# Layer two's second product as seven block products over transposed operands, with the SBUF slots divided by use

## The chip, the cores and the metric

One core of one Trainium2 chip runs the kernel. The metric is device time in microseconds (us) for one execution; lower is better. A profile of one execution gives the rows below. PE is TensorE, DVE is VectorE, ACT is ScalarE, POOL is GpSimd, SP is the engine that issues most DMAs. A "512 matmul" streams 512 columns through a 128x128 weight block.

## The reference

```python
x = attention(q, k_pooled, v_pooled)               # (8, 8, 576, 64) -> 4608 x 512
h = x @ w_in                                       # w_in 512 x 2048
x = (h * (1 / (1 + exp(-1.702 * h)))) @ w_out      # layer one, w_out 2048 x 512
out = ((x @ w_a) * (x @ w_b)) @ w_out2             # layer two, w_a, w_b 512 x 1536, w_out2 1536 x 512
```

Everything is FP32. Each product is made of three matmuls in the rounded FP32 format fp32r: every operand is split in a high part and a low remainder (hi, lo), and hi·hi, hi·lo and lo·hi are summed in PSUM.

## The kernel before

**Units and passes.** The 4608 tokens are nine blocks of 512. Four pairs of blocks and the last block by itself make five units u = 0..4. Work goes through passes i over the hidden columns; in a pass all units are done one after the other. The first phase (attention and a direct layer one) is followed by passes that do layer one with block products, and then by the last three passes, LP, LP+1 and LP+2, which are layer two. Each of these takes four chunks f of 128 hidden columns (f0 to f3 below), of the 12 that there are.

**The first product of layer two** is done in seven block products for eight. The four quarters of x of a unit are combined beforehand into seven operands `xo` (hi and lo, in DRAM as `yd`), the weights of each chunk into seven blocks `wc` (in DRAM as `wd`). `products` runs, for a unit and a chunk, P1, P5, P6, P3, P7, P2, P4, six matmuls each (L837), into PSUM tiles X (two buffers), Y and Z. ACT copies the sums of P1, P5 and P6 out, DVE adds those of P3, P7, P2 and P4, and multiplies the two halves of the gate: L866 after P7 gives column half 1, L871 after P4 column half 0. L814 (ACT) and L815 (DVE) split these into hi and lo.

**The second product** is direct. `out_rows` takes 128 tokens as the stationary operand and a weight tile `wo` (512 columns) as the moving one, three matmuls (L751, L752, L753) per 128 tokens and chunk, into an accumulator of the pool `acc`. These groups stand in a list; an entry On in a table (FIRST_F for a pass's first chunk, OTHER_F) lets n of them run between two products. The first half of them can run while the first product of the next chunk goes on; those of column half 0 run at the end of the pass, during the next unit.

**Sums over passes.** LP writes its part of the result to DRAM (`part`), LP+1 reads and rewrites it, LP+2 reads it and stores the output. So READS holds LP+1 and LP+2. `evict` copies an accumulator out (L941 on ACT, L943 on DVE) or adds the loaded part (L933, DVE), and stores it (L944): by SP in READS, by POOL in LP.

**Order.** The order on PE is fixed by the program (`after_last`). On the other engines a scheduler decides it from its own estimates before the run, and each engine then executes its list strictly in that order.

**Weights of layer two** are converted on the way (`pieces_ab`, `whole`: ACT L1088, DVE L1089 to L1106, then a split and a store). The chunks needed in pass LP+1 are made during LP, those of LP+2 during LP+1, with 512 KB loads on SP.

**Slots.** One pool of 19 slots of 1 MB, tag "w", holds xo, wc, wo, raw words and results in the making.

## Time and profile before

| what | value |
|---|---|
| median of three runs | 1736.1 us (1735.93 to 1737.71) |
| span of the profiled execution | 1732.5 us |
| median of the runs less that span | 3.6 us |
| PE busy | 1717.8 us, 99% of the span |
| DVE busy | 1055.2 us, 61% |
| ACT busy | 682.9 us, 39% |
| POOL busy | 38.5 us, 2% |
| HBM traffic over the span | 247 GB/s |

The span runs from the first to the last instruction of the profiled execution. What a run takes beyond it is start and end of the program, 3.6 us with the median. Busy shares are means over stages with different limits.

### The profile page before, as it was taken

How to read it: one execution, taken by the hardware profiler on the slowest of the kernel's cores; microseconds unless marked ns; L12 is line 12 of the kernel's file. 1: busy time of each engine (PE TensorE's matmuls, PEld its weight loads, DVE VectorE, ACT ScalarE, POOL GpSimd, SP SyncE). 2: the span in 40 equal slices, each digit the busy share in tenths (PEclk: the TensorE clock that was granted, in tenths of full speed). 3: DMA queues.
4: the chain of work that ended last, by engine and by line, in shares of the span. 5: the costliest groups of instructions: out<-in, count | busy, mean ns of one | idle time of the engine just before them, and what ended most of it. 6: DMA issues, size and time to landing. Idle time of an engine off the chain costs nothing.

```text
span 1732.5 us, 23390 instructions
## 1 busy us (share of the span) xinstructions
PE 1717.8 (99%) x8708; PEld 1435.9 (83%) x8708; DVE 1055.2 (61%) x1791; ACT 682.9 (39%) x1624; POOL 38.5 (2%) x69
## 2 busy tenths in 40 slices
PE   9999999999999999999999999999999999999999
PEld 8888887888888888888888888888888888888888
DVE  8999866675846644665555547643547753444443
ACT  8977643553323344544542223322223222222111
POOL 0000000000100000000000100000000000000000
PEclk9999999999999999999999999999999999999999
DMA  7776566465936994756868756598556879735612
GB/s 295 244 272 242 173 213 240 158 240 199 353 125 265 373 377 169 285 193 220 322 237 349 276 201 256 229 373 324 219 214 221 339 298 411 281 123 213 243 58 89
DMA packets 122913, 429.35 MB, mean 248 GB/s; under 512 B 12976, under 2 KB 17584, under 8 KB 99888
## 3 DMA queue, kind: packets, MB, share of 16 engines
q1 hardware_dynamic: 116320, 401.39, 62.5%
q0 software_dynamic: 6480, 26.48, 4.0%
q8 instruction: 68, 1.11, 0.3%
q14 instruction: 45, 0.37, 0.1%
HBM read 286.52 MB, written 141.30 MB: 247 GB/s over the span
## 4 chain that ended last, share of the span: by engine, by line
PE 87%; DVE 6%; DMA 4%; ACT 3%; issue 1%; SPq 0%; ACTq 0%; DVEq 0%
PE X L837 20%; PE Y L837 10%; PE acc L753 6%; PE acc L751 6%; PE acc L752 6%; PE Z L837 5%; PE h L338 4%; PE acc L338 4%; PE acc L340 4%; PE acc L339 4%; PE h L339 4%; PE h L340 4%; PE acc L767 2%; PE acc L766 2%; PE acc L765 2%; DMA yd<-st 2%
## 5 line engine op out<-in xcount | busy, mean ns | idle before, releaser
L837 PE MATMUL X<-xo,wc 128*128 128x512 f32 (+1 forms) x1800 | 410.1, 368 | 1.7 <-ACT s L845 1.7
L837 PEld LDWEIGHTS X<-xo,wc 128*128 128x128 f32 x1800 | 318.7, 188 | 62.6 <-ACT s L845 3.2
L837 PE MATMUL Y<-xo,wc 128*128 128x512 f32 (+1 forms) x900 | 209.2, 368 | 0.0
L837 PEld LDWEIGHTS Y<-xo,wc 128*128 128x128 f32 x900 | 159.2, 188 | 28.6
L851 DVE TENSOR_TENSOR s<-s,Y 128x512 f32<-128x512 f32 (+1 forms) x75 | 47.5, 634 | 169.8 <-PE Y L837 169.6
L338 PE MATMUL h<-x,w 128*128 128x512 f32 x360 | 143.1, 399 | 3.3 <-ACT x L615 2.8
L814 ACT CAST ghi<-s 128x512 fp32r<-128x512 f32 (+1 forms) x90 | 52.0, 578 | 234.3 <-DVE s L866 204.8
L339 PE MATMUL h<-x,w 128*128 128x512 f32 x360 | 140.3, 390 | 0.2 <-DVE x L617 0.2
L339 PE MATMUL acc<-glo,w 128*128 128x512 f32 x360 | 140.3, 390 | 0.2 <-DVE glo L1275 0.2
L340 PE MATMUL h<-x,w 128*128 128x512 f32 x360 | 140.4, 390 | 0.0
L340 PE MATMUL acc<-ghi,w 128*128 128x512 f32 x360 | 140.3, 390 | 0.0
L338 PE MATMUL acc<-ghi,w 128*128 128x512 f32 x360 | 131.6, 398 | 0.4 <-ACT ys L1297 0.3
L814 ACT CAST hi<-s 128x512 fp32r<-128x512 f32 (+1 forms) x90 | 51.5, 578 | 147.0 <-DVE s L871 146.6
L837 PE MATMUL Z<-xo,wc 128*128 128x512 f32 (+1 forms) x450 | 104.5, 368 | 0.0
L571 ACT ACTIVATE at<-sc,mx 128x72 f32<-128x72 f32 x288 | 88.5, 345 | 24.9 <-DVE mx L564 24.8
L837 PEld LDWEIGHTS Z<-xo,wc 128*128 128x128 f32 x450 | 80.0, 188 | 14.8
L753 PE MATMUL acc<-wo,glo 128*128 128x512 f32 x216 | 84.4, 391 | 0.6 <-DVE glo L815 0.6
L751 PE MATMUL acc<-wo,ghi 128*128 128x512 f32 x216 | 84.5, 391 | 0.0
L752 PE MATMUL acc<-wo,hi 128*128 128x512 f32 x216 | 84.3, 390 | 0.0
L751 PE MATMUL acc<-wo,hi 128*128 128x512 f32 x216 | 84.3, 390 | 0.0
L752 PE MATMUL acc<-wo,ghi 128*128 128x512 f32 x216 | 84.3, 390 | 0.0
L753 PE MATMUL acc<-wo,lo 128*128 128x512 f32 x216 | 84.0, 389 | 0.0
(116 smaller groups left out, 3027.0 us busy)
## 6 DMA issues: line engine op xcount, KB each, us to landing
xo<-yd SPq DMA_DIRECT2D x84, 1024.0 KB, 9.1
yd<-st SPq DMA_DIRECT2D x126, 256.0 KB, 3.0
part<-part SPq DMA_DIRECT2D x108, 256.0 KB, 5.0
part<-part SPq DMA_DIRECT2D x19, 1024.0 KB, 7.7
xd<-x SPq DMA_DIRECT2D x18, 1024.0 KB, 7.5
xm<-xd SPq DMA_DIRECT2D x32, 512.0 KB, 8.2
raw<-in_moe_w_out_dram SPq DMA_DIRECT2D x28, 512.0 KB, 7.9
wd<-ws SPq DMA_DIRECT2D x12, 1024.0 KB, 4.1
```

Source lines behind the costliest of these rows:

```text
L338: nc.tensor.matmul(out=o, lhsT=whi, rhs=xhi, start=first, stop=False),
L339: nc.tensor.matmul(out=o, lhsT=whi, rhs=xlo, start=False, stop=False),
L340: nc.tensor.matmul(out=o, lhsT=wlo, rhs=xhi, start=False, stop=last),
L571: pin("ACT", nc.scalar.activation(out=a[:, h, :], in_=sc[:, c, :], func=AF.Exp, bias=mx[:, h:h + 1], accum_out=sm[:, h:h + 1],))
L751: after_last(nc.tensor.matmul(out=oa, lhsT=chi[:, ts], rhs=whi, start=first, stop=False))
L752: after_last(nc.tensor.matmul(out=oa, lhsT=chi[:, ts], rhs=wlo, start=False, stop=False))
L753: after_last(nc.tensor.matmul(out=oa, lhsT=clo[:, ts], rhs=whi, start=False, stop=last))
L765: after_last(nc.tensor.matmul(out=oa, lhsT=whi, rhs=chi, start=first, stop=False))
L766: after_last(nc.tensor.matmul(out=oa, lhsT=wlo, rhs=chi, start=False, stop=False))
L814: nc.scalar.copy(out=chi, in_=src)
L837: after_last(nc.tensor.matmul(out=banks[nm], lhsT=w[we][:, ks], rhs=x[:, xe, kk, :], start=n in FIRST and kk == 0 and m == 0, stop=kk == 1 ...
L851: made = nc.vector.tensor_tensor(out=s[2], in0=s[2], in1=Y, op=ALU.add)
```

## The change

The second product of layer two is computed transposed: the weights are stationary, the tokens are the moving side, and it goes through seven block products as well, now over pairs p of chunks. A unit has 14 groups, two for each product (one per pair of chunks), called k0 to k13 here. Each group computes two accumulators (r = 0, 1) with three matmuls each: 84 matmuls for a unit, of 512 columns, or 256 for the last unit, instead of 96 (48) of 512. The tokens' side of a group is made by `ready`: four subtractions on DVE for each pair of chunks, and a split (ACT cast, DVE subtract) for each group. The weights' side is made with the other weights (seven blocks, `wd["o", n]`).

The running sums of the block products are read in the middle: after each odd k, `add_out` (L954; in LP the first time L952, a copy on ACT) adds the two accumulators to a quarter of the result, and a later group goes on accumulating in the same PSUM banks: k4 continues in the two banks of Y that are read after k3, k8 in those of X that are read after k1. The additions after k7, k9, k11 and k13 end a quarter each, which is then stored by ACT's own DMA queue. In a unit that is 14 additions, 8 subtractions and 14 splits on DVE.

Other parts of the change: the next unit's xo are loaded as soon as their slot is free, at the end of each product of f3 (`load_operand`), instead of earlier into other slots; parts are loaded in quarters (`load_quarter`, L945: column 1 of rows 2 and 3 in f2, column 0 and column 1 of rows 0 and 1 in f3, the last two after k7); 126 stores of `yd` go from SP to POOL; weights of chunks 0 to 4 are made in the first phase, those of 5 to 11 one quarter at a time by `made_late`, with POOL loads and stores through two small tiles `spare`, spread from LP's second chunk to the end of LP+1; the 19 slots become 14 of "w", 4 of "wo", 1 of "v". The result is stored transposed and turned outside the kernel.

```diff
-ROOM = dict(ps=4, acc=3, at=2, aT=4, tmp=2, g=1, gg=2, ks=4, raws=2, vs=2, q=2, xs=3, raw=2, yp=2, w=19)
+ROOM = dict(ps=4, acc=3, at=2, aT=4, tmp=2, g=1, gg=2, ks=4, raws=2, vs=2, q=2, xs=3, raw=2, yp=2, w=14, wo=4, v=1)
...
-            t = wp.tile([P, 2, 2, N], F32R, tag="w", name="xo")
+            t = big("v" if i == L2 - 1 and n == 0 else "w", [P, 2, 2, N], F32R, "xo")
...
-    def out_rows(i, f, col, ti, j, c, first, last):
...
-        whi, wlo = w[:, f % 2, :], w[:, 2 + f % 2, :]
-        ts = slice(ti * P, (ti + 1) * P)
...
-        after_last(nc.tensor.matmul(out=oa, lhsT=chi[:, ts], rhs=whi, start=first, stop=False))
-        after_last(nc.tensor.matmul(out=oa, lhsT=chi[:, ts], rhs=wlo, start=False, stop=False))
-        after_last(nc.tensor.matmul(out=oa, lhsT=clo[:, ts], rhs=whi, start=False, stop=last))
...
+                if not one_ and u + 1 < NU2:
+                    load_operand(i, u + 1, USED.index(o))
...
-                held[1, f] = col_tiles(gp, 2, "ghi", "glo")
-                parts(held[1, f], s[1])
+                held[i, u, f, 1] = s[1]
...
+        if last and not one_:
+            ready, sweep_ = sweep(i, u)
...
+            elif what[0] == "L":
+                for c, col in LOADED[what] if i in READS else ():
+                    load_quarter(i, u, c, col)
...
-        groups.extend(g for _, g in rows_of(1, f, held.pop((1, f))))
         if last:
-            per_f = [list(rows_of(0, f_, held.pop((0, f_)))) for f_ in fs]
-            for ti in range(n_ // P):
-                groups.extend(p[ti][1] for p in per_f)
...
+    SWEEP = (1, 5, 3, 2, 6, 7, 4)
+    ADDS = {1: (0, 0), 5: (1, 1), 3: (0, 1), 2: (0, 0), 6: (0, 1), 7: (1, 1), 4: (1, 0)}
+    ENDS = (2, 6, 7, 4)
...
+            for to, x, y in {3: (((0, 0), (0, 1), (0, 0)),),
+                             4: (((0, 1), (1, 1), (0, 1)), ((1, 1), (1, 1), (0, 0))),
+                             6: (((1, 0), (1, 0), (1, 1)),)}.get(o, ()):
+                nc.vector.tensor_tensor(out=b(*to), in0=b(*x), in1=b(*y), op=ALU.subtract)
+            e, col = ((0, 0), (1, 0), (1, 1), (0, 0), (1, 1), (0, 1), (1, 0))[o]
+            xs[k_] = pair_tiles(n_, (k_ if final else made_ops[0]) % ahead < 2)
+            made_ops[0] += 1
+            split(*xs[k_], b(e, col))
...
+            for r in range(2):
+                if n in (1, 5) and k_ % 2 == 0:
+                    banks[bank_, r] = acc.tile([P, n_], F32, tag="acc", name="acc")
+                o_ = banks[bank_, r]
+                whi, wlo = (wo[:, e, r * P:(r + 1) * P] for e in range(2))
+                for m, (w_, x_) in enumerate(((whi, hi), (whi, lo), (wlo, hi))):
+                    after_last(nc.tensor.matmul(
+                        out=o_, lhsT=w_, rhs=x_, start=n in FIRST and k_ % 2 == 0 and m == 0,
+                        stop=k_ % 2 == 1 and m == 2, skip_group_check=True,
+                    ))
+                if k_ % 2:
+                    add_out(i, u, 2 * row + r, col, o_, n in ENDS)
...
+            ready(k_ + ahead)
+            if k_ == 7 and i in READS:
+                load_quarter(i, u, 2, 0)
+                load_quarter(i, u, 3, 0)
+            if u == NU2 - 1 and i + 1 < L2 and k_ in (3, 7, 11, 13):
+                load_o(i + 1, k_ // 4)
...
+    LOADED = {"L1": ((2, 1), (3, 1)), "L2": ((0, 0), (1, 0)), "L3": ((0, 1), (1, 1))}
...
+    def add_out(i, u, c, col, a, done):
+        j, cols = place_of(u, col)
+        t = part_t.get((i, u, c, col))
+        if t is None:
+            t = part_t[i, u, c, col] = out_tile(c, col, cols.stop - cols.start)
+            nc.scalar.copy(out=t, in_=a)
+        else:
+            nc.vector.tensor_tensor(out=t, in0=a, in1=t, op=ALU.add)
+        if done:
+            part_t.pop((i, u, c, col))
+            to = part[2][j][:, c, cols] if i in WRITES else out[c * P:(c + 1) * P, j * N + cols.start:j * N + cols.stop]
+            ended.append(op(nc.scalar.dma_start, to, t))
...
-            nc.sync.dma_start(out=yd[u][:, o, e, kk] if w_ == N else yd[u][:, o, e], in_=f32(ts[e]))
+            nc.gpsimd.dma_start(out=yd[u][:, o, e, kk] if w_ == N else yd[u][:, o, e], in_=f32(ts[e]))
...
-    FIRST_F = ("O2", "P1", "O2", "P5", "O2", "P6", "O2", "P3", "O1", "P7", "O2", "P2", "O3", "P4")
-    OTHER_F = ("P1", "P5", "O1", "P6", "P3", "O1", "P7", "O1", "P2", "O3", "P4")
+    FIRST_L2 = ("O5", "P1", "O5", "P5", "O5", "P6", "O6", "P3", "O7", "O8", "P7", "P2", "P4")
+    TABLES = (
+        ("P1", "P5", "O1", "P6", "O1", "P3", "P7", "O1", "P2", "O1", "P4"),
+        ("O1", "P1", "P5", "O1", "P6", "P3", "O1", "P7", "P2", "O1", "P4"),
+        ("O1", "P1", "P5", "O1", "P6", "P3", "O1", "P7", "P2", "O1", "L1", "P4"),
+        ("P1", "O1", "P5", "P6", "O1", "L2", "P3", "P7", "P2", "L3", "P4"),
+    )
...
+    def pieces_late(key, source):
+
+        def load(n):
+            raws[key, n] = spare()
+            nc.gpsimd.dma_start(out=as_words(raws[key, n].bitcast(U32)), in_=source(1 - n // 2, n % 2))
+
+        def make(n):
+            if n == 0:
+                vs2[key] = big("v", [P, 8, 2 * P], F32, "v")
+            whole(as_words(raws.pop((key, n)).bitcast(U32)), vs2[key][:, n])
+
+        def store(c):
+            v, n = vs2[key], min(2, 7 - c)
+            lo = v[:, 1 + c:1 + c + n]
+            hi = spare().bitcast(F32R).rearrange("p (c n) -> p c n", c=2)[:, 0:n]
+            nc.scalar.copy(out=hi, in_=lo)
+            nc.vector.tensor_tensor(out=lo.bitcast(F32R), in0=lo, in1=f32(hi), op=ALU.subtract)
+            for e, t in enumerate((f32(hi), lo)):
+                nc.gpsimd.dma_start(out=wd[key][:, c:c + n, e], in_=t)
+
+        return [op(load, 0), op(load, 1)] + [
+            o for n in range(4) for o in [op(make, n, cost=1.6)] + ([op(load, n + 2)] if n < 2 else [])
+        ] + [op(combine, key, cost=1.4)] + [op(store, c, cost=.5) for c in range(0, 7, 2)]
...
+    spread_late(
+        made_late(range(EARLY, NF2)), place[LP, 0, passes[LP][1][1]], place[L2 - 2, NU2 - 1, passes[L2 - 2][1][0]] - 3,
+    )
```

**PE, where k4 follows k3.** The rows are PE's in pass LP+2, unit 1, from the end of chunk f0: k3 (L905, `hi`), product P4 (L782, X) and k4 (L905, `ghi`).

```order
L905 MATMUL acc<-hi,wo 128x512 x2
L905 MATMUL acc<-lo,wo 128x512
L905 MATMUL acc<-hi,wo 128x512
L782 MATMUL X<-xo,wc 128x512 [waits DMAHW6_49,DVE_49]
L782 MATMUL X<-xo,wc 128x512 x5
L905 MATMUL acc<-ghi,wo 128x512 [waits DMAHW1_49,DVE_49,Activation_49]
L905 MATMUL acc<-glo,wo 128x512
L905 MATMUL acc<-ghi,wo 128x512
L905 MATMUL acc<-ghi,wo 128x512 [waits DVE_49]
L905 MATMUL acc<-glo,wo 128x512
L905 MATMUL acc<-ghi,wo 128x512
```

Before, chunk f0 of the same unit ended with three groups of `out_rows` (L751 to L753), P4 and the next chunk's P1, which follow P4 in one row:

```order
L751 MATMUL acc<-wo,hi 128x512
L752 MATMUL acc<-wo,hi 128x512
L753 MATMUL acc<-wo,lo 128x512
L751 MATMUL acc<-wo,hi 128x512 [waits DVE_49]
L752 MATMUL acc<-wo,hi 128x512
L753 MATMUL acc<-wo,lo 128x512
L751 MATMUL acc<-wo,hi 128x512
L752 MATMUL acc<-wo,hi 128x512
L753 MATMUL acc<-wo,lo 128x512
L837 MATMUL X<-xo,wc 128x512 [waits DMAHW6_49,DVE_49]
L837 MATMUL X<-xo,wc 128x512 x11
```

Where P1 followed P4 without a wait, k4 now follows it, and each of its two accumulators has a wait for DVE ahead of its first matmul.

**DVE, the same place.** The rows go from P2's sum (L803) past k1's two additions, the product after P4 (L817), a split, and k3's two additions with a subtraction between them.

```order
L803 TENSOR_TENSOR s<-s,Z 128x512 [waits PE_49]
L954 TENSOR_TENSOR part<-acc,part 128x512 [waits DMAHW3_49,DMAHW1_49,PE_49]
L954 TENSOR_TENSOR part<-acc,part 128x512 [waits DMAHW4_49,DMAHW2_49,PE_49]
L817 TENSOR_TENSOR s<-s,X 128x512 [waits DVE_49,PE_49]
L305 TENSOR_TENSOR glo<-s,ghi 128x512 [waits Activation_49]
L954 TENSOR_TENSOR part<-acc,part 128x512 [waits DMAHW1_49,DMAHW0_49]
L882 TENSOR_TENSOR s<-s 128x512 [waits DVE_49]
L954 TENSOR_TENSOR part<-acc,part 128x512 [waits DMAHW3_49,DMAHW1_49]
```

The same stretch of before: the gate's product after P7 (L866), a split, P2's sum (L856), an addition, the product after P4 (L871), a split.

```order
L866 TENSOR_TENSOR s<-s 128x512 [waits DVE_49]
L815 TENSOR_TENSOR glo<-s,ghi 128x512 [waits Activation_49]
L856 TENSOR_TENSOR s<-s,Z 128x512 [waits PE_49]
L933 TENSOR_TENSOR part<-acc,part 128x512 [waits DMAHW4_49,DMAHW2_49,PE_49]
L871 TENSOR_TENSOR s<-s,X 128x512 [waits DVE_49,PE_49]
L815 TENSOR_TENSOR lo<-s,hi 128x512 [waits Activation_49]
```

Where one addition stood between P2's sum and the product after P4, two now do, and two more follow that product, the last of them seventh behind P2's sum.

**SP, loads for the unit after.** The rows are SP's in pass LP+2 as unit 0 ends: the last xo loads of unit 1 (`yd_92`) and the first of unit 2 (`yd_93`), each waiting for PE to free its slot, then parts; the first two, from `part_0`, are what k1's additions add to.

```order
L415 DMA xo<-yd_92 128x2048 [waits DMAHW4_49,PE_49]
L415 DMA xo<-yd_92 128x2048 [waits DMAHW5_49,PE_49]
L415 DMA xo<-yd_92 128x2048 [waits DMAHW6_49,PE_49]
L415 DMA xo<-yd_93 128x2048 [waits DMAHW7_49,PE_49]
L945 DMA part<-part_0_134 128x512 [waits DMAHW1_49,DMAHW0_49,DVE_49]
L945 DMA part<-part_0_134 128x512 [waits DMAHW3_49,DVE_49]
L945 DMA part<-part_0_134 128x512 [waits DMAHW4_49,DMAHW2_49,DVE_49]
L945 DMA part<-part_0_134 128x512 [waits DMAHW5_49,DMAHW3_49,DVE_49]
```

Before, parts of the same unit stood ahead of the xo loads, which came two chunks earlier:

```order
L924 DMA part<-part_1_135 128x512 [waits DMAHW7_49]
L924 DMA part<-part_1_135 128x512 [waits DMAHW0_49]
L924 DMA part<-part_0_134 128x512 [waits DMAHW2_49,DMAHW1_49]
L924 DMA part<-part_0_134 128x512 [waits DMAHW4_49]
L428 DMA xo<-yd_92 128x2048 [waits DMAHW3_49,PE_49]
L428 DMA xo<-yd_92 128x2048 [waits PE_49]
L428 DMA xo<-yd_92 128x2048 [waits DMAHW5_49,PE_49]
L428 DMA xo<-yd_92 128x2048 [waits DMAHW6_49,PE_49]
L428 DMA xo<-yd_93 128x2048 [waits DMAHW7_49,PE_49]
L428 DMA xo<-yd_93 128x2048 [waits DMAHW0_49,PE_49]
```

The parts that k1's additions read have moved from ahead of the xo loads to behind the last of them.

## Rows read from the trace of the kernel before

**Rows 1.** The profile's page: busy time by engine, and the granted clock in 40 slices.

```profile
PE 1717.8 (99%) x8708; PEld 1435.9 (83%) x8708; DVE 1055.2 (61%) x1791; ACT 682.9 (39%) x1624; POOL 38.5 (2%) x69
...
PEclk9999999999999999999999999999999999999999
```

**Rows 2.** The chain of work that ended last: start, length, what.

```profile
1154.21 1.43 PE X L837 x12
...
1369.47 2.72 PE X L837 x12
```

**Rows 3.** The waits of PE: us in total, times, longest.

```profile
PE X L837 <- ACT s L845: 1.7, 3, 0.7
...
PE acc L753 <- DVE glo L815: 0.6, 3, 0.2
```

**Rows 4.** Groups of instructions by line and shape: busy us, mean ns | idle before.

```profile
L751 PE MATMUL acc<-wo,ghi 128*128 128x512 f32 x216 | 84.5, 391 | 0.0
...
L815 DVE TENSOR_TENSOR glo<-s,ghi 128x512 fp32r<-128x512 f32 x72 | 49.6, 688 | 14.4 <-ACT ghi L814 14.3
...
L933 DVE TENSOR_TENSOR part<-acc,part 128x512 f32<-128x512 f32 x72 | 49.1, 690 | 51.7 <-PE acc L753 51.4
...
L845 ACT COPY s<-X 128x512 f32<-128x512 f32 x60 | 35.2, 586 | 40.1 <-PE X L837 38.3
```

**Rows 5.** DVE in time, where it works without a pause, in LP+1.

```profile
1353.25 1.28 DVE L933 TENSOR_TENSOR part<-acc,part 128x512 f32<-128x512 f32 x2
1354.45 0.68 DVE L1100 TENSOR_TENSOR v<-v,raw 128x512 f32<-128x512 f32 x1
1355.05 0.68 DVE L815 TENSOR_TENSOR lo<-s,hi 128x512 fp32r<-128x512 f32 x1
```

**Rows 6.** Windows in LP+1, in LP+2 and around LP's last unit.

```profile
core 0: us, PE busy (x) PEld busy (x) DVE busy (x) ACT busy (x) POOL busy (x), PEclk, DMA share, GB/s
1300.00:1360.00 60.00, 60.00 (x266) 49.65 (x265) 47.67 (x85) 20.04 (x31) 0.00 (x0) 1.00 0.74 278
1500.00:1560.00 60.00, 60.00 (x266) 49.67 (x265) 25.33 (x38) 12.48 (x21) 0.00 (x0) 1.00 0.55 203
1154.00:1186.00 32.00, 31.80 (x201) 28.51 (x201) 10.67 (x25) 8.23 (x21) 2.56 (x5) 1.00 1.00 400
```

**Rows 7.** DMA issues: count, KB each, median us from issue to landing.

```profile
xo<-yd SPq DMA_DIRECT2D x84, 1024.0 KB, 9.1
yd<-st SPq DMA_DIRECT2D x126, 256.0 KB, 3.0
part<-part SPq DMA_DIRECT2D x108, 256.0 KB, 5.0
...
part<-ys POOLq DMA_DIRECT2D x36, 256.0 KB, 6.8
```

**Rows 8.** The seven xo loads of one unit in LP (line L428).

```profile
L428 SPq DMA_DIRECT2D xo<-yd x7: 319/320/566, 1067.8 to 1077.1; - x7
...
DMA to landing us min/median/max: 7.5/11.2/16.2
```

**Rows 9.** Raw weight words in layer two: who waited (us, times).

```profile
  ACT v L1088: 13.9, 13
```

**Rows 10.** The end of the program in time.

```profile
1719.54 0.88 PE L837 MATMUL Z<-xo,wc 128*128 128x256 f32 x6
1719.74 0.42 DVE L865 TENSOR_TENSOR s<-s,X 128x256 f32<-128x256 f32 x1 [0.92 <-PE X L837]
...
1720.25 0.94 PE L837 MATMUL X<-xo,wc 128*128 128x256 f32 x6
...
1721.57 0.42 DVE L815 TENSOR_TENSOR glo<-s,ghi 128x256 fp32r<-128x256 f32 x1
...
1722.04 0.50 PE L753 MATMUL acc<-wo,glo 128*128 128x512 f32 x1 [0.20 <-DVE glo L815]
...
1728.72 0.69 DVE L933 TENSOR_TENSOR part<-acc,part 128x512 f32<-128x512 f32 x1 [2.03 <-PE acc L753]
```

More of the change, by code (lines that the diff above doesn't have):

```diff
@@ L630, in tile_kernel @@
     raw_t = {}
-    tmps = []
     def as_words(t):
@@ new lines, in tile_kernel, with load_o, out_tile @@
+    made_ops = [0]
+    wo_t = {}
+    def load_o(i, m):
+        t = wo_t[i, m] = big("wo", [P, 4, 2, 2 * P], F32R, "wo")
+        for k_ in range(4 * m, min(4 * m + 4, 14)):
+            nc.sync.dma_start(
+                out=f32(t[:, k_ % 4]), in_=wd["o", passes[i][1][0] // 2 + k_ % 2][:, PRODUCTS[SWEEP[k_ // 2]][0]]
+            )
+    LOADED = {"L1": ((2, 1), (3, 1)), "L2": ((0, 0), (1, 0)), "L3": ((0, 1), (1, 1))}
+    def out_tile(c, col, n_):
+        if col == 0:
+            return yp.tile([P, n_], F32, tag="y", name="part")
+        return p2.tile([P, n_], F32, tag="part", name="part", bufs=4)
@@ L902, in tile_kernel, with load_part @@
     part_t = {}
-    def load_part(j):
-        part_t[j] = wp.tile([P, KD, N], F32, tag="w", name="part")
+    def load_part(j, tag="w"):
+        part_t[j] = big(tag, [P, KD, N], F32, "part")
         nc.sync.dma_start(out=part_t[j], in_=part[1][j])
     def load_rows(i, u, col):
-        one_ = passes[i][0] == 3
-        n_ = N if len(units[u]) == 2 or not one_ else HALF
-        for ti in range(4 if len(units[u]) == 2 or one_ else 2):
+        for ti in range(4):
+            j, cols = place_of(u, col)
+            n_ = cols.stop - cols.start
@@ L1148, in made @@
             if f % 2 == 0:
-                ops += pieces_o(f // 2, [rows("o2", f + e) for e in range(2)])
+                key = "o", f // 2
+                ops += [op(load_raw_o, key, e) for e in (1, 0)] + pieces_ab(key, (None, None))[2:]
             ops += pieces_ab(f, [columns("a", f), columns("b", f)])
@@ L1215, in tile_kernel, with first_o @@
     spread_late(
-        mixed_x(4) + made(range(FB)),
+        mixed_x(4) + made(range(EARLY)),
         place[1, 0, FIRST_FS[0]], place[1, J5, FA] - 2,
     )
-    for i in (LP, LP + 1):
-        f = passes[i + 1][1]
-        spread_late(made(f), place[i, 1, passes[i][1][0]], place[i, NU2 - 1, passes[i][1][0]] - 3)
+    spread_late(
+        made_late(range(EARLY, NF2)), place[LP, 0, passes[LP][1][1]], place[L2 - 2, NU2 - 1, passes[L2 - 2][1][0]] - 3,
+    )
+    def first_o(m):
+        load_o(LP, m)
+    before[LP, 0, passes[LP][1][2]] = [op(first_o, m) for m in range(4)]
     for i in range(L1, L2):
@@ L1224, in tile_kernel @@
         if i > L1:
-            before.setdefault((i - 1, NU2 - 1, passes[i - 1][1][0]), []).extend(loads(i))
+            ops, at_ = loads(i), passes[i - 1][1]
+            if passes[i - 1][0] == 3:
+                cuts = [len(ops)]
+            else:
+                cuts = CUTS
+            for n, (a, b) in enumerate(zip([0] + cuts, cuts)):
+                key = (i - 1, NU2 - 1, at_[n]) if n < len(at_) else (i, 0, fs[0])
+                before.setdefault(key, []).extend(ops[a:b])
         else:
```

245 lines of the change are left out of this document (128 added, 117 removed), and 4 rows, old and new, of the table ENDING.

## The prediction

> **What bounds the kernel now.** I read the page first: PE is busy 99% of the span, its granted clock is full in every slice, and no other engine is above 61% [rows 1]. The chain that ended last agrees: it runs almost wholly through PE's matmuls, as pieces such as twelve 512 matmuls in 2.72 us, which is 0.2267 us each, or twelve 256 matmuls in 1.43 us, 0.119 each [rows 2]. PE's waits then say what is left besides: in layer two its largest entries are 1.7 and 0.6 us in total [rows 3]. So before, the time of layer two is the number of matmuls times their pace. A matmul removed is time saved, and any new wait of PE is lost in full. I therefore price the removed matmuls first, and then look for waits.
>
> **Matmuls.** Each of the six groups of the second product has 216 matmuls of 512 columns [rows 4], 1296 in all; at 0.2267 that is 293.8 us. After, four pairs in three passes with 84 each make 1008 of 512 columns, 228.5 us, and the single unit 252 of 256 columns, 30.0 us. The difference is **-35.3 us**. A pair unit falls from 264 to 252 matmuls, from 59.8 to 57.1 us.
>
> **k4 waits for k3's additions.** k4 adds to the PSUM banks that DVE must first have read after k3, and only one product, P4, stands between the two on PE. No row of before shows such a wait, so I walk DVE's list with its own times. A 512 operation starts 0.60 us after the one ahead of it (1353.25, two of them, 1354.45, 1355.05) and takes 0.69 [rows 5, 4]. It starts 0.20 us after PE moves on from the tile that it reads (1719.54 to 1719.74), and PE starts 0.05 us after a DVE result (1721.57 + 0.42 to 1722.04) [rows 10]. A slot of six 512 matmuls is 1.36 us. In LP+2, unit 1, with 0 at the start of f0's P1: the table puts P2 at 10.9 to 12.2, k3 at 12.2 to 13.6, P4 at 13.6 to 15.0, and PE wants k4 at 14.96. On DVE, P2's sum starts at 12.7, as two subtractions and a split are ahead of it; k1's two additions take until 14.5. The product after P4 can't start before 14.96 + 0.20 = 15.16. Behind it stand a split (15.76), k3's first addition (16.36 to 17.05), a subtraction and k3's second (17.56 to 18.25). So k4 starts at 17.1 instead of 14.96, and its second accumulator, due 0.68 us later, another 0.5 us late: 2.7 us for this unit. The same walk through the other places of LP+1 and LP+2 gives 0.7 to 3.8 us each and, over nine of them, **+18 us**. In LP the first additions are ACT copies of 0.59 us [rows 4] in another list, and I find no loss. Bounds: 5 us if DVE runs ahead of my walk wherever a split could be overlapped, 30 if every place costs as much as the worst (3.8 on eight pairs).
>
> **Parts behind the xo loads.** k1's additions read parts whose loads now stand on SP behind the last xo load, which waits for the end of P4 in f3 (time 0 in the walk). They cost nothing as long as they land by 13.96, since two additions then still end before 15.16; behind that, k4 is late by as much. The stream ahead of them starts when f3's P1 is done, at -10.9, and has 7 MB; the parts of k1 add 0.5 MB. At the 400 GB/s of the window around LP's last unit [rows 6] that is 2.6 us per MB, and with some 2 us for the first landing all are there at 10.6. Before, the seven loads of one unit in LP were issued from 1067.8 to 1077.1, the quickest took 7.5 us, the slowest 16.2 [rows 8]: 6 MB in some 18.0 us, 3.0 per MB, beside other loads and stores. With that start and that pace the parts land at 16.1, 2.1 late. LP+1 has weights in the making beside it, LP+2 has not: I take 1.0 us for each of LP+1's four pairs, nothing in LP+2: **+4 us**, bounds 0 and 17 (2.1 on eight pairs).
>
> The Trainium skill, DMA: Bandwidth & Descriptors, section "Queues, rings and completion order", says that a DMA engine takes turns between the queues that it has work for. By that rule each MB that POOL or ACT moves beside the stream delays it by 2.6 us; with about 0.8 MB of weights and 0.5 MB of result stores beside it, the parts would land at some 14.0 and this term would be nothing. The slow landings of POOL and xo in the trace [rows 7, 8] agree with shared engines, and no row shows the share.
>
> **DVE's load.** A pair unit had 36 DVE operations of 512 columns and now has 56: at 0.60, 33.6 of 57.1 us. Weights in the making add about 12 us a key, a key in some 45 us, thus 15: 49 of 57, 85%. Before, DVE was busy 47.67 of 60 us in a window of LP+1, without a pause of PE [rows 6]. I add nothing beyond the walk, which has these operations where they lie on its way. If the cover went, it would show as more of the same waits.
>
> **Weights through POOL.** Ten keys are made with loads and stores of POOL through two small tiles, so ACT, the first to touch raw words, waits for a POOL load or store some five times a key. Before, ACT waited 13.9 us in 13 places for raw words in layer two [rows 9], at no cost to PE [rows 3]. What hides such a wait is ACT's slack: P6 needs a buffer of X that P1's copy has to leave, and has 2.72 us for a copy of 0.59 and about 0.25 of hand-over: 1.9 us. A POOL DMA of 256 KB took 6.8 us at the median [rows 7], but the list was ordered with DMA times in mind, so only the excess is waited for. **+2.5 us**, bounds 0 and 40 (50 waits at 0.8 beyond the slack).
>
> **The rest.** 126 stores of `yd` on POOL instead of SP: the tiles they hold come free later (3.0 us on SP, 6.8 on POOL [rows 7]), but SP no longer has them between loads; with the changes between passes, **+1.0**, bounds 0 and 6. DMA issues on ACT have no row; eight a unit at a few tenths each fit into ACT's 61% of idle time [rows 1]. At the end, before, the last product stands at 1720.25, the span ends 12.2 us later, 8 of it matmuls, then an addition and a store [rows 10]. After it now come 14 groups of 0.71 us with bank reads among them that nothing covers: the matmuls are in the first term, for the waits **+1.3**. SBUF slots and the transposed store cost nothing by themselves: what waits for a slot is in the terms above.
>
> **Sum.** -35.3 + 18 + 4 + 2.5 + 1.0 + 1.3 = -8.5. Against the profiled execution's span, 1732.5, that is 1724.0; the median of the runs lies 3.6 above the span, so I forecast 1727.6.
>
> **The rivals.**
> *Full gain.* DVE keeps up and k4 finds its banks read. For: DVE has idle time on the mean. Against: its order is fixed, and the product after P4 stands ahead of k3's additions. Matmuls, pass changes and end alone: 1736.1 - 35.3 + 2.3 = 1703.
> *Loads late.* xo and parts come late in all eight reading pairs: 2.1 each, 17 instead of 4: 1741. For: every load of the next unit now waits for the last use of its slot, with 10.9 us until it is wanted, while landings took 7.5 to 16.2 us [rows 8]. Against: LP+2 has little traffic beside it, 203 GB/s of 400 [rows 6].
> *ACT held by POOL's weights*, the case on the slower side by itself: the copies of X behind an ACT instruction that waits for a POOL DMA come late, and P3 or P7 with them. It decides from the point where an average wait is above 1.9 us; at 2.4, 50 waits lose 0.5 each, 25 instead of 2.5: 1750. For: POOL's 6.8 us [rows 7], two tiles only. Against: the 13.9 us before that cost nothing [rows 9].
>
> **How the numbers follow.** Forecast 0.45, with its own range 1718 to 1733; full gain 0.15; loads late 0.18; ACT held 0.22. The range reaches from near the full gain to just beyond ACT held: 1706 to 1752. 0.2%, 3.5 us, is about what a measurement of this kernel can tell from no change. Faster by more: the full gain and nearly all of the forecast, 0.60. Slower by more: ACT held and a part of the late loads, 0.26. The rest, 0.14.
>
> **What would show it.** Right: PE's waits gain an entry of second-product matmuls waiting for DVE's additions, 14 to 22 us, in LP+1 and LP+2 and hardly in LP; matmul time 35 us less; DMA entries among PE's waits under 10 us. Wrong: PE waiting mainly for xo, for ACT's copies of X, or for DVE's own splits; then the pace of loads, POOL's weights or DVE's load was mis-sized.

## The result and the profile after

The changed kernel takes 1751.65 us (median of four, 1747.51 to 1755.05), the kernel before on the same chip 1736.3. The ratio is 1.0086, interval 1.0067 to 1.0104: 15 us slower, where 8.5 us faster was forecast. The profiled execution took 1754.29 us, with a span of 1752.5, 20.0 above that of before.

From the page of the kernel after, busy time by engine:

```profile
PE 1702.0 (97%) x8672; PEld 1417.7 (81%) x8672; DVE 1235.6 (71%) x2251; ACT 747.6 (43%) x1782; POOL 166.0 (9%) x282
...
PE 70%; DMA 11%; DVE 7%; issue 7%; ACT 3%; POOL 2%; SPq 0%; POOLq 0%; DVEq 0%; ACTq 0%
```

Against [rows 1], PE is at 97% instead of 99%, and the second line, the chain by engine, has DMA in it with 11%. PE's busy time fell by 15.8 us only, not by the 35.3 of the removed matmuls; the mean granted clock says part of why:

```profile
core 0: 1752.5 us, clock 0.993
```

0.007 of 1752.5 are some 12 us of clock that was not granted, and PE counts as busy while it runs slowly. What PE waited for (line, releaser: us in total, times, longest):

```profile
PE X L782 <- DMA xo<-yd: 8.5, 8, 2.0
PE Y L782 <- DMA wc<-wd: 5.4, 1, 5.4
PE Y L782 <- DMA xo<-yd: 5.3, 5, 2.3
PE acc L905 <- DVE part L954: 5.0, 7, 1.9
PE X L782 <- DVE s L812: 4.2, 2, 4.1
```

L782 are the matmuls of the first product (L837 before), L905 those of the second. In [rows 3] the largest entry in layer two was 1.7. Operands now come late: xo 14 us in all, and one wc 5.4.

Where the time went follows from the starts of the units' first matmuls. Layer two begins 7.3 us later than before (first a row of before, then of after; start, length, what):

```profile
904.47 0.86 PE L837 MATMUL X<-xo,wc 128*128 128x512 f32 x3
```

```profile
911.82 1.55 PE L782 MATMUL X<-xo,wc 128*128 128x512 f32 x6
```

From there to the last matmul it takes 837.1 us instead of 823.8: 13.3 more, so that 48.6 were lost beside the 35.3 that were saved. A pair unit with 252 matmuls and no wait is 57.1. Units of the kernel after, as windows (us, busy time and instructions by engine, granted clock, DMA share, GB/s): LP unit 2, LP+1 units 1 and 2, LP+2 unit 2.

```profile
1031.20:1093.20 62.00, 59.31 (x253) 48.24 (x252) 42.84 (x86) 23.70 (x44) 10.01 (x16) 0.97 0.57 211
1241.88:1308.31 66.43, 60.42 (x253) 48.00 (x252) 52.23 (x108) 21.27 (x40) 13.65 (x21) 0.97 0.69 257
1308.31:1374.47 66.16, 59.76 (x253) 47.83 (x252) 50.18 (x104) 20.03 (x37) 9.26 (x15) 0.97 0.71 269
1579.90:1637.02 57.12, 57.12 (x254) 47.30 (x252) 36.83 (x57) 15.35 (x26) 0.00 (x0) 1.00 0.54 203
```

The unit of LP+2 has the whole gain: 57.12 us, PE busy in all of it. In the others, where POOL works on the late weights (its busy time is the sixth figure), 5 to 9 us are lost. Summed in this way, each unit against its matmuls:

| place | lost, us |
|---|---|
| LP, unit 0, chunk f3 (16.95 instead of 9.52) | 7.4 |
| LP, units 1 to 3 | 15.1 |
| LP+1, units 1 to 3 | 20.3 |
| LP+2, units 1 to 3 | 0.9 |
| LP+2, unit 4 with the second products that run in it (54.7 instead of 49.0) | 5.7 |

Four waits in the timeline (start, length, what, idle before it). The first, in LP's unit 0:

```profile
951.76 0.32 SPq L1274 DMA_DIRECT2D wc<-wd  x1
...
957.17 2.93 PE L782 MATMUL Y<-xo,wc 128*128 128x512 f32 x6 [5.45 <-DMA wc<-wd]
```

The load of f3's second wc block was issued only when a slot of "w" came free, after f3 had begun, and PE stood 5.45 us. The second and third are waits for xo in f0, ahead of P7, 11.35 us after the start of units 2 and 3 of LP:

```profile
1042.55 2.81 PE L782 MATMUL X<-xo,wc 128*128 128x512 f32 x6 [2.00 <-DMA xo<-yd]
1104.55 1.63 PE L782 MATMUL X<-xo,wc 128*128 128x512 f32 x6 [2.01 <-DMA xo<-yd]
```

Six 512 matmuls took 2.81 us behind the one wait and 1.63 behind the other. The fourth, in LP+1, goes from a POOL load to PE over ACT and DVE:

```profile
1369.74 0.43 ACT L1132 ACTIVATE v<-spare 128x256 f32<-128x256 f32 x1 [6.35 <-DMA spare<-in_moe_w_a_dram]
1370.20 0.29 DVE L1133 TENSOR_SCALAR v<-v 128x256 f32<-128x256 f32 x1 [2.54 <-ACT v L1132]
1371.01 0.68 DVE L812 TENSOR_TENSOR s<-s,X 128x512 f32<-128x512 f32 x1
1371.74 4.64 PE L782 MATMUL X<-xo,wc 128*128 128x512 f32 x10 [4.06 <-DVE s L812]
```

ACT waits for raw words, DVE stands behind ACT's result, and the addition after P7, behind that in DVE's list, releases a bank of X 4.06 us late. This is the only stall of this kind of that size.

The granted clock (seventh figure) around these waits and two others:

```profile
950.00:960.00 10.00, 4.55 (x15) 3.36 (x14) 8.50 (x20) 4.27 (x9) 3.26 (x6) 0.69 0.84 295
970.00:980.00 10.00, 8.82 (x30) 6.66 (x30) 3.54 (x6) 4.33 (x8) 2.90 (x4) 0.83 1.02 424
1040.00:1050.00 10.00, 8.00 (x29) 6.18 (x28) 5.58 (x9) 1.33 (x3) 0.00 (x0) 0.83 0.61 252
1260.00:1270.00 10.00, 8.11 (x29) 6.25 (x28) 7.99 (x14) 2.48 (x5) 3.38 (x7) 0.83 0.34 122
1370.00:1380.00 10.00, 8.26 (x25) 6.59 (x26) 7.78 (x19) 3.03 (x7) 0.00 (x0) 0.66 1.02 422
```

One less the clock, times 10 us, is 3.1 + 1.7 + 1.7 + 1.7 + 3.4 = 11.6 us in these five stretches: nearly all of the 12. Not all of it is time lost: the granted clock was low from 953.90, while PE stood until 957.17, and from 1370.32, while it stood until 1371.74. Over the time in which PE worked it comes to 9.6 us.

The 35.4 us that the pairs of LP and LP+1 lost divide, by PE's waits in these units and the granted clock behind them, so:

| what | us |
|---|---|
| waits for xo | 13.4 |
| slow clock behind two of them (from 970.96 and 1042.64) | 3.4 |
| the stall behind ACT (4.06) and its slow clock | 6.8 |
| waits for the additions L954 (2.2) and the slow clock behind one | 3.9 |
| other waits for ACT (v 1.8, a copy 0.5) | 2.3 |
| in no wait of the list; 4.6 of it in chunks f0 with waits for xo | 5.6 |

How the xo loads stand, in LP+1's unit 2 for its successor, then in LP+2's unit 2:

```profile
L415 SPq DMA_DIRECT2D xo<-yd x7: 319/320/320, 1296.9 to 1308.5; - x7
...
  PE Y L782: 1.3, 2
  PE X L782: 1.0, 2
...
DMA to landing us min/median/max: 7.4/13.1/16.2
```

```profile
L415 SPq DMA_DIRECT2D xo<-yd x7: 319/320/320, 1569.2 to 1580.1; - x7
...
DMA to landing us min/median/max: 7.8/10.1/13.5
```

Both are issued over 11 us, product by product, as the slots come free. With the late weights beside them they land in up to 16.2 us and PE waits; without, in 13.5, and nobody waits. Before, the slowest took 16.2 us too [rows 8], but all seven were issued before the unit that reads them began, at 1081.62, and PE did not wait: what is new is that the loads have no slack.

### The profile page after: what moved, and what is told of

Read it like the earlier page. It is cut to its first block, busy times and chain, and to the rows that moved or that the text cites. A ratio compares the mean times of both kernels' runs of the same rounds, so it can differ in the third digit from the quotient of the medians.

```text
span 1752.5 us, 24466 instructions
## 1 busy us (share of the span) xinstructions
PE 1702.0 (97%) x8672; PEld 1417.7 (81%) x8672; DVE 1235.6 (71%) x2251; ACT 747.6 (43%) x1782; POOL 166.0 (9%) x282
## 4 chain that ended last, share of the span: by engine, by line
PE 70%; DMA 11%; DVE 7%; issue 7%; ACT 3%; POOL 2%; SPq 0%; POOLq 0%; DVEq 0%; ACTq 0%
PE X L782 16%; PE acc L905 12%; PE Y L782 8%; DMA xo<-yd 5%; PE h L323 4%; PE h L324 4%; PE acc L323 4%; PE h L325 4%; PE acc L325 4%; PE acc L324 4%; PE Z L782 4%; POOL yd L994 2%; PE px L589 1%; ACT at L558 1%; PE sc L542 1%
## 5 line engine op out<-in xcount | busy, mean ns | idle before, releaser
L782 PE MATMUL X<-xo,wc 128*128 128x512 f32 (+1 forms) x1800 | 420.3, 373 | 16.9 <-DMA xo<-yd 8.5
L782 PEld LDWEIGHTS X<-xo,wc 128*128 128x128 f32 x1800 | 320.1, 190 | 82.7 <-issue 11.8
L782 PE MATMUL Y<-xo,wc 128*128 128x512 f32 (+1 forms) x900 | 213.2, 373 | 12.1 <-DMA wc<-wd 5.4
L782 PEld LDWEIGHTS Y<-xo,wc 128*128 128x128 f32 x900 | 160.1, 191 | 44.7 <-DMA xo<-yd 6.1
L304 ACT CAST ghi<-s 128x512 fp32r<-128x512 f32 (+1 forms) x137 | 79.9, 583 | 242.1 <-PE acc L905 188.7
L905 PE MATMUL acc<-ghi,wo 128*128 128x512 f32 (+1 forms) x548 | 179.3, 372 | 2.1 <-DVE part L954 2.1
L305 DVE TENSOR_TENSOR glo<-s,ghi 128x512 fp32r<-128x512 f32 (+1 forms) x137 | 87.7, 640 | 71.1 <-ACT ghi L304 70.6
L954 DVE TENSOR_TENSOR part<-acc,part 128x512 f32<-128x512 f32 (+1 forms) x170 | 104.9, 634 | 46.1 <-PE acc L905 43.7
L905 PEld LDWEIGHTS acc<-ghi,wo 128*128 128x128 f32 x548 | 101.9, 189 | 21.5 <-issue 2.4
L782 PE MATMUL Z<-xo,wc 128*128 128x512 f32 (+1 forms) x450 | 104.7, 368 | 0.3 <-DMA xo<-yd 0.3
L905 PE MATMUL acc<-glo,wo 128*128 128x512 f32 (+1 forms) x274 | 102.0, 372 | 0.0
L792 ACT COPY s<-X 128x512 f32<-128x512 f32 (+1 forms) x75 | 40.8, 544 | 143.3 <-PE X L782 125.7
L905 PE MATMUL acc<-hi,wo 128*128 128x512 f32 (+1 forms) x292 | 94.0, 368 | 3.1 <-DVE part L954 2.9
L994 POOL DMA_DIRECT2D yd<-st x126 | 67.9, 542 | 253.2 <-ACT st L304 199.3
L782 PEld LDWEIGHTS Z<-xo,wc 128*128 128x128 f32 x450 | 79.5, 188 | 14.9 <-DVE s L813 0.7
```

What stands on the lines that cost most here:

```text
L304: nc.scalar.copy(out=hi, in_=src)
L305: (nc.vector.tensor_tensor(out=lo, in0=src, in1=f32(hi), op=ALU.subtract))
L782: after_last(nc.tensor.matmul(out=banks[nm], lhsT=w[we][:, ks], rhs=x[:, xe, kk, :], start=n in FIRST and kk == 0 and m == 0, stop=kk == 1 ...
L792: nc.scalar.copy(out=st(0), in_=X)
L905: after_last(nc.tensor.matmul(out=o_, lhsT=w_, rhs=x_, start=n in FIRST and k_ % 2 == 0 and m == 0, stop=k_ % 2 == 1 and m == 2, skip_grou ...
L954: nc.vector.tensor_tensor(out=t, in0=a, in1=t, op=ALU.add)
```

## The experiments

The theories. **A**: the xo loads, 7 MB within f3 and early f0, are late because the late weights' DMAs share the engines with them. The rivals: **B**, ACT is held by instructions that wait for their DMAs; **C**, the slots alone make xo late, whatever the traffic; **D**, the late weights' arithmetic fills ACT and DVE; or the `yd` stores on POOL are to blame. "Lost" is a pair unit's length over 57.1. A "key" is one set of late weights, those of a chunk (5 to 11) or, for the second product, of a pair of chunks ("o3" to "o5"): ten in all. Ratios are to the kernel before on the same chip. In the diffs, "..." stands for code left out.

**No late weights.**

```diff
-            nc.sync.dma_start(out=f32(slots_[k][:, at_:at_ + n]), in_=wd[key][:, c:c + n])
+            nc.sync.dma_start(out=f32(slots_[k][:, at_:at_ + n]), in_=wd[key if passes[i][0] == 3 else key % 4][:, c:c + n])
...
-    spread_late(
-        made_late(range(EARLY, NF2)), place[LP, 0, passes[LP][1][1]], place[L2 - 2, NU2 - 1, passes[L2 - 2][1][0]] - 3,
```

> No weights are made during LP and LP+1; the chunks that would have used them read those of chunks 0 to 3 instead, so the output is not the reference's. Theory A (xo loads are late because each can only be issued at the last use of its slot and then shares the DMA engines with the weights in the making) and theory B (ACT is held by instructions that wait for POOL's DMAs) both expect LP+1's pairs u1 and u2 to fall from 66 us to 57 to 58, as in LP+2, and the whole to some 1725. Theory C (the slots alone: loads issued at the last use are late whatever goes on beside them) expects LP+1 to stay within 3 us of 66 and the whole above 1743.

1728.97 us, ratio 0.9953 (0.9937 to 0.997): 23 us under the kernel after. LP's units 1 to 3 lose 2.7, 0 and 0 us instead of 15.1 together, LP+1's 3.9, 0.9 and 0.6 instead of 20.3. PE's waits:

```profile
PE Y L782 <- DMA wc<-wd: 5.5, 1, 5.5
PE h L323 <- ACT x L602: 4.5, 2, 2.6
PE Y L782 <- DMA xo<-yd: 3.2, 3, 1.5
PE acc L905 <- DVE part L954: 2.7, 5, 1.1
...
PE X L782 <- DMA xo<-yd: 2.4, 5, 0.8
```

The late weights cost most of the loss, and C is out as its main cause; the wait for wc is there without them, and LP's and LP+1's first pairs still lose 6.6 us. Layer two still starts late, at 914.8.

**Their DMAs alone.** Loads from finished weights, stored again without arithmetic.

```diff
+        def store(n):
+            t, c = raws.pop((key, n)).rearrange("p (c n) -> p c n", c=2), 2 * n
+            for e in range(2):
+                nc.gpsimd.dma_start(out=wd[key][:, c:min(c + 2, 7), e], in_=t[:, 0:min(2, 7 - c)])
```

> The late weights' DMAs stay (four loads of 256 KB and 1.75 MB of stores a key, by POOL), the arithmetic on ACT and DVE goes, and nothing reads what is stored; the weights that are read are those of chunks 0 to 3, so the output is not the reference's. Theory A expects PE to wait for xo as in the changed kernel, 10 us or more in LP and LP+1, and a time of 1738 to 1748. Theory B expects hardly more than without late weights at all, within 4 us of that run.

1752.4 us, 1.0097 (1.0077 to 1.0117), yet it tells nothing of A: with no arithmetic to wait for, POOL ran ahead of the program. Its 120 late DMAs began at 519.5, and 112 of them started before layer two did, whose start moved to 930.8, 16 us later than without late weights. LP's units 0 and 1 were 3.8 and 3.5 us longer than there (the last late DMA started at 1001); from LP's unit 2 on the pairs were like those without late weights.

**The same, paced.** Each load is held by a one-column write of DVE in its place in the program.

```diff
             raws[key, n] = spare()
+            nc.vector.memset(raws[key, n][:, 0:1], 0.0)
```

> The late weights' DMAs without their arithmetic, as in the run before, but now each load waits for a one-column fill on DVE that stands where the arithmetic stood, so that the traffic lies in LP and LP+1 and not before; the output is not the reference's. Theory A expects 1743 to 1752, with LP+1's u1 and u2 above 64 us. Theories B and D expect 1727 to 1734, with these two below 61 us.

1750.02 us, 1.0093 (1.0071 to 1.0114). Its waits, and its units 1 and 2 of LP+1:

```profile
PE X L782 <- DMA xo<-yd: 10.2, 9, 2.7
PE Y L782 <- DMA xo<-yd: 9.3, 5, 3.8
```

```profile
1240.03:1307.39 67.36, 60.79 (x253) 48.94 (x252) 36.61 (x64) 15.32 (x26) 13.88 (x22) 0.95 0.72 253
1307.39:1368.63 61.24, 58.78 (x253) 48.23 (x252) 35.98 (x61) 15.34 (x26) 9.23 (x15) 0.97 0.71 258
```

DVE has 36.6 us of work in a unit instead of 52.2, and unit 1 loses as much as with it (66.43); unit 2 is 4.9 us shorter, as the stall behind ACT isn't there, so that it falls below the 64 us that A had expected. The traffic alone costs 21 us over the kernel without late weights by the medians, 24 by the ratios.

**The arithmetic alone.** POOL fills the raw tiles by itself; no stores.

```diff
-            nc.gpsimd.dma_start(out=as_words(raws[key, n].bitcast(U32)), in_=source(1 - n // 2, n % 2))
+            nc.gpsimd.memset(raws[key, n], 1.0)
...
-                nc.gpsimd.dma_start(out=wd[key][:, c:c + n, e], in_=t)
```

> The late weights' arithmetic on ACT and DVE stays, POOL fills the small tiles with a constant instead of loading words, and nothing is stored; the weights read are those of chunks 0 to 3, so the output is not the reference's. Theory A (their DMA traffic makes xo late) and theory B (ACT is held because it waits for POOL's loads and stores) both expect about the time without late weights, 1727 to 1733. Theory D (the arithmetic itself overloads DVE and ACT) expects 1743 or more.

1730.95 us, 0.9975 (0.9964 to 0.9985): 2 us above the kernel without late weights by the medians, 4 by the ratios. With the run before it, D is out and A is shown in the main: nearly all that the late weights cost is their DMAs. How much of it is xo is less sure: paced, the waits for xo were 19.5 us, in the kernel after 13.8 by the same two lines, and there B has a part, 6.8 us in the stall behind ACT and 1.8 behind v.

**`yd` stores back on SP.**

```diff
-            nc.gpsimd.dma_start(out=yd[u][:, o, e, kk] if w_ == N else yd[u][:, o, e], in_=f32(ts[e]))
+            nc.sync.dma_start(out=yd[u][:, o, e, kk] if w_ == N else yd[u][:, o, e], in_=f32(ts[e]))
```

> The 126 stores of yd go on SP again. If POOL's queue makes them late, the 7 us lost before layer two (904.5 to 911.8) shrink to under 2 and LP's first two pairs get shorter, 1740 to 1745 in all. If it does not matter who issues them, the start of layer two stays at 911 or so and the time within 3 us of 1751; SP's xo loads may even come later behind them.

1751.04 us, 1.0085 (1.0066 to 1.0103): no difference in all; layer two started at 909.5, still 5 us late.

**More slack for one xo.** Without late weights, the first xo of the next unit goes to slot "v" in every pass.

```diff
-            t = big("v" if i == L2 - 1 and n == 0 else "w", [P, 2, 2, N], F32R, "xo")
+            t = big("v" if passes[i][0] == 2 and n == 0 else "w", [P, 2, 2, N], F32R, "xo")
```

> As the run without late weights, and the slot that these used takes the first xo of each unit in LP and LP+1 too, as it does in LP+2. If what is left of the waits for xo there comes from having no slot free, this is 4 to 10 us faster than the run without late weights; if traffic alone made them late, the two are within 2 us.

1749.19 us, 1.0074 (1.0059 to 1.0089). The slot was held by a part at LP's start, so that layer two began at 942.6, 28 us later. The wait for wc went (f3 of unit 0: 9.52), and units 1 of LP and LP+1 fell to 57.3 and 58.0, from 59.8 and 61.0. From its start on, layer two took 799.3 us instead of 809.5 without the edit. So what is left without late weights comes in the main from the slots: a load that may start earlier is not late, but the slot was not there to give.

**Unit 4's parts in a slot "wo".**

```diff
-            homes = ("wo", "v") if len(units[u]) == 2 else ("w",)
+            homes = ("wo", "v") if len(units[u]) == 2 else ("wo",)
```

> The last unit's part of layer one's sum goes into a wo slot instead of a w slot. If the wait of 5.4 us for wc in LP's first unit comes from the w slots being full (14 for seven xo, seven wc and this part), it goes and the time falls by 5 to 8 us. If the load is late for another cause, the wait stays and the time is within 2 us of the changed kernel's.

1769.95 us, 1.0204 (1.0177 to 1.0231). The wait for wc is gone again, and a larger one stands at LP's start:

```profile
PE acc L713 <- DVE part L728: 24.9, 2, 23.9
```

The shortage moved to "wo".

**Late loads one chunk ahead of their reader**, so that ACT might find them landed.

```diff
-        return [op(load, 0), op(load, 1)] + [
+        return [[op(load, 0), op(load, 1)], [op(make, 0), op(load, 2), op(make, 1), op(load, 3)],
+                [op(make, 2), op(make, 3)], [op(combine, key)] + [op(store, c) for c in range(0, 7, 2)]]
...
```

> The same work as the changed kernel, but each late load is put a chunk (about 14 us) ahead of the instruction that reads it, a key in three chunks. Theory B expects ACT's waits for POOL's DMAs to nearly vanish and the time to fall to 1734 to 1744. Theories A and D expect no change beyond 3 us, as traffic and arithmetic are the same.

1748.99 us, 1.0083 (1.0065 to 1.01): the same. PE waits 8.6 us for xo and a new 4.4 for ACT's copies (L794). But the edit did not do what it was for: ACT's waits for the late DMAs in layer two, 40.3 us in the kernel after, are 39.5 here. So this run says nothing against B; against B as the main cause stand the paced run, in which ACT has no part in the late weights, and PE's own list of waits.

**Late weights at f0 and f1 of each unit**, away from the xo loads.

```diff
...
+    at_steps = [(LP, 0, 1, 0, 2)] + [(LP, u, 0, u, 1) for u in range(1, NU2)] + [
+        (LP, NU2 - 1, 3, -1, 0), (LP + 1, 0, 1, 0, 2)] + [(LP + 1, u, 0, u, 1) for u in range(1, NU2 - 1)]
...
```

> All work of the changed kernel is done; only the late weights are placed so that their loads and stores fall into chunks f0 (its end), f1 and f2 of a unit, away from f3 and the start of f0, where xo loads run. Theory A (their traffic beside the xo loads) expects PE's waits for xo in LP and LP+1 to fall from 14 to under 7 us and the time to 1733 to 1742. If the amount of traffic in a whole unit matters and not its place, or if DVE gets too full in f1 and f2, it stays at 1746 or above.

1751.34 us, 1.0087 (1.0061 to 1.0114). Of the 2.72 us that a pair was to gain on the kernel before, LP's units 2 and 3 have 2.63 and 1.78. In LP+1's pairs POOL still moved 1.1 to 1.8 MB beside the xo, as stores slid into f3 and the next f0, and all three lose; PE's waits for xo are 15.1 us in all, not under 7.

**LP's weights at f0 and f1 of units 1 to 4, the others where they don't meet the loads.**

```diff
...
+    at_steps = {5: (LP, 1, 0, 1), 6: (LP, 2, 0, 1), 7: (LP, 3, 0, 1), "o3": (LP, 4, 0, 1), "o4": (LP, 4, 3, 4),
+                8: (LP + 1, 0, 1, 2), 9: (LP + 1, 0, 3, 4), 10: (LP + 1, 1, 3, 4), 11: (LP + 1, 2, 3, 4), "o5": (LP + 1, 4, 0, 1)}
...
```

> All work of the changed kernel is done. As in the run before, but no key is made in LP's first unit, and in LP+1 each key's stages stand one chunk earlier, since there the stores had slid into f3 and f0. Theory A expects POOL's traffic beside the xo loads under 1 MB in LP's u2 and u3 and LP+1's u2 and u3, their f0 at 16.3 to 17.5 us, and the time at 1731 to 1740. If the place of the traffic does not matter, f0 stays at 18 to 21 us in LP+1 and the time at 1746 or above; if DVE or ACT get too full in f0 and f1, PE waits for ACT's copies or DVE's sums there instead.

1775.49 us, 1.0231 (1.0211 to 1.0252). LP's units 1 to 3 are 1.08, 2.61 and 1.34 shorter than in the kernel before, LP+1's 6.0, 4.9 and 1.2 longer; 28.3 us more are a wait of this edit's own, as LP+2's first xo needs the slot "v" that the last weights held.

**The same for LP, and the rest spread evenly.**

```diff
...
+    at_steps = {5: (LP, 1, 0, 1), 6: (LP, 2, 0, 1), 7: (LP, 3, 0, 1), "o3": (LP, 4, 0, 1)}
...
+    spread_late(rest_, place[LP, 4, passes[LP][1][2]], place[L2 - 2, NU2 - 1, passes[L2 - 2][1][0]] - 3)
```

> All work done. LP's four keys stand as in the run before (f0 and f1 of u1 to u4), the other six are spread evenly from the end of LP to the end of LP+1 as in the changed kernel, none in LP+1's last unit, so that no xo load waits for the slot of the making. Theory A expects LP to keep its gain (its pairs within 1.5 us of 57.1) and the time to be 1738 to 1746; if the gain in LP was luck of that run's order, LP's pairs are 60 us or more again.

1751.74 us, 1.0092 (1.0069 to 1.0115). LP keeps its gain (59.0, 57.2 and 58.2 us; the first is more than 1.5 above 57.1). Its unit 2, which took 62.00 in the kernel after:

```profile
1026.93:1084.14 57.21, 57.21 (x253) 47.22 (x252) 40.70 (x81) 22.59 (x42) 7.61 (x12) 1.00 0.58 212
```

POOL moves its weights in this unit and PE never stops: with its DMAs at another time, the loss is gone. But six keys then fall to the end of LP and to LP+1: LP+1's units 3 and 4 and LP+2's unit 0 take 3.2, 5.9 and 2.7 us more than in the kernel after, its unit 1 still 66.0, and the median is unchanged.

**Late weights' DMAs on SP**, and then this with the edit ahead.

```diff
-            nc.gpsimd.dma_start(out=as_words(raws[key, n].bitcast(U32)), in_=source(1 - n // 2, n % 2))
+            nc.sync.dma_start(out=as_words(raws[key, n].bitcast(U32)), in_=source(1 - n // 2, n % 2))
...
-                nc.gpsimd.dma_start(out=wd[key][:, c:c + n, e], in_=t)
+                nc.sync.dma_start(out=wd[key][:, c:c + n, e], in_=t)
```

> The changed kernel with one edit: the late weights' loads and stores are issued by SP instead of POOL. Behind xo loads in SP's own queue they should not take turns with them. If sharing between the queues is what makes xo late, PE's waits for xo in LP and LP+1 fall from 14 to under 8 us, 1738 to 1746. If only the bytes beside the xo loads count, the time is within 3 us of 1751; if SP itself is held by stores that wait for ACT and DVE, xo loads are issued late and it is slower than 1754.

1745.06 us, 1.0055 (1.0036 to 1.0073), some 6 us better by the medians; the interval still touches that of the kernel after (1.0067 to 1.0104).

> The two runs before in one: LP's keys in f0 and f1, and all late DMAs on SP. If both help by themselves, 1732 to 1740; if SP is held by stores waiting for ACT and DVE, slower than the one on POOL.

1746.56 us, 1.0061 (1.0042 to 1.008): no better than SP by itself. In the first of the two PE's waits for xo are 12.3 us, not under 8. LP's unit 3 has f0 at 16.32 us, no loss, with some 1.2 MB of late weights beside its xo; on POOL 1.65 MB beside it made 19.63. But LP's unit 2 has 18.42 with 1.0 MB, where four of the late stores stood ahead of six of the seven xo loads on SP, and LP+1's unit 3 has 22.82. The Trainium skill, DMA: Bandwidth & Descriptors, section "Queues, rings and completion order", says that a DMA engine takes turns between the queues that it has work for; by that rule late weights behind xo in xo's own queue would not delay it. LP's unit 3 agrees; as the late DMAs mostly stood between and ahead of the xo loads, this run is no test of the rule.

**Fewer weights early.** No late weights, and chunk 4 and the third block of the second product's weights are not made in the first phase either.

```diff
-    HELD, EARLY = FM - FA, FB + 1
+    HELD, EARLY = FM - FA, FB
```

> As the run without late weights (1729), and chunk 4's weights and the third block of the second product's weights are not made in the first phase either; the output is not the reference's. If the 7 to 10 us that layer two starts later (904.5 before, 911.8 after, 914.8 without late weights) come from this extra making on ACT and DVE, layer two starts 4 to 9 us earlier and the time is 1720 to 1725. If they come from the scheduler's other order or from POOL's stores of yd, it stays within 2 us of 1729.

1723.37 us, 0.9923 (0.9901 to 0.9944). Layer two starts at 909.6 instead of 914.8: these weights cost 5.2 us ahead of it. So some 13 us under the kernel before is what the shorter product gives once the late weights and these two are left out, work that a complete kernel has to do somewhere.

## Why the prediction was wrong

Two steps failed. The largest cost of the sum, k4's wait, was read out of an order of DVE that the list did not have; and the arrival of xo, the slots, the clock and the start of layer two, which took back the whole gain, stood in the sum at 4 us or at nothing. The prediction's own sign of being wrong came: PE waits mainly for xo.

**Matmuls, -35.3: right.** LP+2's unit 2 is 57.12 us, as worked out, and 59.84 before.

**k4 waits for k3's additions, +18: the step that failed first, by a misread order.** All of L905's waits for L954 are 5.0 us, 2.2 of it in the pairs: k4 waited in two of the nine places (1.89 and 0.33 us, in LP+1's units 1 and 3). The timeline of LP+2, unit 1:

```profile
1535.88 0.68 DVE L803 TENSOR_TENSOR s<-s,Z 128x512 f32<-128x512 f32 x1
...
1536.35 1.52 PE L782 MATMUL X<-xo,wc 128*128 128x512 f32 x6
1536.47 1.28 DVE L954 TENSOR_TENSOR part<-acc,part 128x512 f32<-128x512 f32 x2
...
1537.71 0.39 PE L905 MATMUL acc<-ghi,wo 128*128 128x512 f32 x1
...
1537.91 0.69 DVE L817 TENSOR_TENSOR s<-s,X 128x512 f32<-128x512 f32 x1 [0.16 <-PE X L782]
...
1540.54 0.69 DVE L954 TENSOR_TENSOR part<-acc,part 128x512 f32<-128x512 f32 x1
```

The two additions ahead of the product after P4 are k3's, those behind it k1's, which PE needs only for k8; the section on the change and the walk have them the other way round. k4 starts at 1537.71, 1.36 after P4's start, without a wait; had those behind been k3's, it could not have started before 1540.54. DVE's list had shown it: the first two had a wait for PE, behind P2's sum that had one too, which only a result later than P2, k3's, needs; the later ones had none.

**Parts behind the xo loads, +4: wrong with it.** They feed k1's additions, which nothing waits for soon. What was late is the xo stream ahead of them. The step had its pace at 3.0 us per MB from [rows 8] (in the pairs of LP and LP+1 the seven landed 2.9 to 3.5 us apart), but looked at its end only: the first product takes the seven operands within 13.6 us of f0's start, 2.3 us apart on the mean, so that a stream of 3 us per MB needs a lead at its start, and where it had none it was late on the way.

**Loads late: the rival with the right mechanism** in the wrong place. It took the parts and xo together, at 2.1 us in all eight pairs of LP+1 and LP+2, 17 in all. It is xo, in LP and LP+1: of the 35.4 us that their pairs lost, 16.8 are waits for xo and the slow clock behind two of them, and up to 4.6 more stand in the same chunks. LP+2 lost 0.9.

**The wait for wc and the slots: the sum left them out.** "SBUF slots ... cost nothing by themselves" cost 7.4 us in LP's unit 0 (5.45 of wait, the rest nearly all slow clock), and made each xo wait for its predecessor's last use.

**The clock: left out.** 9.6 us of PE's time, all behind waits of 1.9 to 5.5 us; they are within the other terms.

**Weights through POOL, +2.5, and the rival ACT held.** PE stood behind raw words on ACT once for 4.06 us, 6.8 with the slow clock, and for v (L1132) 1.8 in all; the arithmetic alone costs 2 to 4. The rival gave 1750, close to what was measured, by a mechanism that made little of it: that is luck, and so is it that the stated range, which ends at 1752 because of this rival, reaches the measured time.

**The rest, +1.0.** With the stores of `yd` back on SP the time is the same, so that they are no part of the loss.

**The start, not in the sum.** 7.3 us; fewer weights ahead give back 5.2. What the rest is stays open.

**The end, +1.3: 5.7.** In unit 4 of LP+2 PE waits 2.8 us for L954; matmuls 168 of 256 columns, u3's 84 of 512 and 84 of 256 come to 20.0 + 19.0 + 10.0 = 49.0, and it took 54.7. What the other 2.9 us are stays open.

What is not settled: no version with all the work done came under 1745 us. Whether the ten weights can be placed so that they miss all xo loads and all held slots stays open.

## What to carry to other kernels

Work taken from a saturated engine is time saved only where its operands keep their slack: where a load can start only at its slot's last use, other DMAs in that stretch can be paid for by the engine, so price the stretch in MB, operand by operand, before the total. When two like instructions stand around a third in a list, see from their waits which buffer each one reads before pricing it.
